# Two more places for raw weight pieces in block one of an attention and expert kernel

## The chip, the cores and the metric

One core of a Trainium2 chip runs the kernel. The metric is the device time of one execution in microseconds (us). The kernel before takes 918.38 us, the median of three runs (917.42 to 919.25).

## What is computed

```python
def _attn_ref(q, k, v):                      # B 4, H 8, S 576, D 64
    q_d, k_d, v_d = (mean over groups of 4 tokens)
    out_up = np.repeat(sm_attn(q_d, k_d, v_d), 4, axis=2)
    mask = np.abs(pos[:, None] - pos[None, :]) < 4
    scores = np.where(mask, scale * q @ k^T, -1000000.0)
    return out_up + softmax(scores) @ v

x = attention as 2304 tokens x 512
h = x @ w_in;  g = relu(h) ** 2;    x = g @ w_out      # block one, d_ff 2048
h = x @ w_in2; g = h * np.cos(h);   out = g @ w_out2   # block two, d_ff 2048
```

The weights come as 64-bit floats. Products in float32 accuracy are made on TensorE of a high part (fp32r) and a low part (the rest): high times high, low times high, high times low.

## The kernel before, in words

**Stages.** First an early stage does pooled ("down") and banded ("pair") attention for the first tokens. Then block one runs in five windows j of 460 or 464 tokens and 16 pieces f of d_ff: slot i = 16 j + f. A slot is `stage_a1` (L801: 12 matmuls into the one bank `ps_h`, xh·w1hi, xl·w1hi, xh·loa), then on ScalarE `gt` = relu (L825), square (L826) and `gh` (L813), on VectorE `gl` = gt - gh (L819), and `stage_b1` (L884: 12 matmuls into `acc`, gh·w1hi, gl·w1hi, gh·lob). "Group f" below is the xh·w1hi and xl·w1hi products of slot f, "gl(f)" its low part. Block two follows (L836, L908). The attention tasks for later windows run in between the slots of block one: scores (L564), exponentials (L386), divisions on GpSimd (L491 for pair, L423 for down), transposes (L503, L433), pooling of the next batch from `pl` tiles (VectorE L368 qc, L373 kp, L375 vp).

**Weights of block one.** Each piece (1 MB of raw 64-bit words, w_in and w_out) is converted once, in the first window, by the task `conv1(f)`. It needs a free `raw` tile (two of them, `caps["raw"]`), loads the piece with one DMA on SyncE's queue (L649), and runs `split`: ScalarE reads the top words (L666), VectorE clamps and shifts (L670, L673) and joins them with the low words (L675, the last reader of `raw`, after which the tile is free again), ScalarE rounds to the high part `w1hi` (L684, into tile `hi{f}`), VectorE subtracts for `loa` and `lob` (L691), which SyncE writes to memory for later windows (L719). `conv1(0)` to `conv1(2)` are tasks from the start; `conv1(f)` starts at slot f - 4.

**Tiles lent out.** The 16 tiles `hi0` to `hi15` are empty until their piece is converted. In the early stage hi3 to hi15 serve as staging for attention inputs: `need` and `done` take them from the list `spare` and put them back; `kept` holds a few for bands.

**What sets the order.** A scheduler builds one instruction list for each engine when the program is made; at run time each engine, and SyncE's queue of DMAs, takes its list strictly in order. All loads and writes that matter here stand on SyncE's queue. Tasks take tiles when `advance` steps them, sorted by `RANK` (attention first, conversions last).

Of the kernel before, what the change touches and what calls it, by code (L numbers as in the profile page):

```python
# [8 lines left out]
F32 = mybir.dt.float32  # L9
F32R = mybir.dt.float32r  # L10
BF16 = mybir.dt.bfloat16
U32 = mybir.dt.uint32
# [6 lines left out]
P = 128  # L19
# [40 lines left out]
TOP_MAX = (2.0 - 2.0 ** -3 - 2.0 ** -23) * 2.0 ** 16 * TOP_SCALE  # L60
LO_RING = (("loa", AHEAD), ("lob", AHEAD + LAG))
SPREAD = ("qk0", "pl", "dpr", "dpt")
LENT = {"dpr": "vw", "dpt": "pl"}
PRODUCTS = ((5, 5), (0, 0), (3, 6), (1, 1), (4, 4), (2, 2), (6, 3))
RANK = {"down": 0, "pair": 1, "pool": 2, "conv1": 3, "conv2": 3}
# [27 lines left out]
def kernel(  # L93
# [76 lines left out]
    def done(name, n=1):  # L170
        f = taken[name].pop(0) if early[0] and name in SPREAD else None
        if f is None:
            used[name] -= n
        elif f in caps:
            used[f] -= n
        else:
            spare.append(f)

    spare = list(range(AHEAD, NF))
    kept = [spare.pop() for _ in range(W0[1] // 4 + 1)]  # L180
    held, taken = {}, {}

# [464 lines left out]
    def load_raw(layer, f):  # L647
        raw = rawp.tile([P, 2 * DM, 2], U32, tag="raw", name="raw")
        nc.sync.dma_start(out=raw.rearrange("p c w -> p (c w)"), in_=weights[layer][f])  # L649
        return raw  # L650

    def behind(*names):
        for name in names:
# [5 lines left out]
        return tc.issue_after(last["pe"]) if follows and not early[0] else nullcontext()  # L659

    def split(raw, hi, los=None, sums=None, held_back=None):
        low, top = raw[:, :, 0], raw[:, :, 1]
        x = rawp.tile([P, 2 * DM], U32, tag="bits", name="bits")
        xv = x.bitcast(F32)
        with behind("hi", "xh", "exp"):
            nc.scalar.activation(out=xv, in_=top.bitcast(F32), func=AF.Prelu, scale=TOP_SCALE, alpha=TOP_ALPHA)  # L666
        while held_back and held_back():
            yield
        with behind("pr" if early[0] and not added[0] else "gl", "xl"):
            nc.vector.tensor_scalar(  # L670
                out=xv, in0=xv, scalar1=TOP_MAX, scalar2=-TOP_MAX * TOP_ALPHA, op0=ALU.min, op1=ALU.max
            )
        nc.vector.tensor_scalar(out=x, in0=x, scalar1=3, scalar2=None, op0=ALU.logical_shift_left)  # L673
        yield
        joined = nc.vector.scalar_tensor_tensor(  # L675
            out=x, in0=low, scalar=29, in1=x, op0=ALU.logical_shift_right, op1=ALU.bitwise_or
        )
        if held_back and added[0]:
            last["xl"] = joined.ins
        if sums:  # L680
            yield from sums(xv)
        yield "read"
        with behind("hi", "xh"):
            nc.scalar.activation(out=hi, in_=xv, func=AF.Copy)  # L684
        yield
        if los is None:
            nc.gpsimd.tensor_tensor(out=xv, in0=xv, in1=hi.bitcast(F32), op=ALU.subtract)
        else:
            for k, lo in enumerate(los()):
                cs = slice(k * DM, (k + 1) * DM)  # L690
                nc.vector.tensor_tensor(out=lo, in0=xv[:, cs], in1=hi[:, cs].bitcast(F32), op=ALU.subtract)  # L691
        return xv
# [2 lines left out]
    lo1 = {}  # L695
    
    def conv1(f, after=0):
        yield from need("raw")
        raw = load_raw(1, f)
        yield  # L700
        yield
        while len(ready) < after or len(scored) < 4:
# [7 lines left out]

        waits = {0: lambda: divided[0] < W0[1], 1: lambda: len(ready) < W0[1]}
        for said in split(raw, hi1[f], ring, held_back=waits.get(f) if early[0] else None):
            if said:
                done("raw")
            yield
            while f == 2 and said and now[0] < 1:
                yield
# [12 lines left out]
    def conv2(u):  # L730
# [4 lines left out]
        yield  # L735
        hi = rawp.tile([P, 2 * DM], F32R, tag="shi", name="shi", bufs=1)
        n = 3 * HALF
        rest = raw.rearrange("p c w -> p (c w)")
        total, top = rest[:, :n].bitcast(F32), rest[:, 2 * DM:2 * DM + n].bitcast(F32R)

        def sums(x):
# [540 lines left out]
```

## Time and profile before

| | before |
|---|---|
| median of 3 runs | 918.38 us (917.42 to 919.25) |
| profiled execution, own time | 915.9 us |
| its span | 914.1 us |
| mean granted clock of TensorE | 0.990 |
| busy: TensorE, VectorE, ScalarE, GpSimd | 891.4, 645.6, 573.0, 97.7 us |

The span is the time from the first to the last instruction that the hardware profiler recorded. TensorE is busy nearly throughout; so what counts is each place where it stands still, what released it there, and the clock that it was granted afterwards. A row of the timeline gives, in brackets, the idle time just before an instruction and what ended it.

### The profile page before, as it was taken

The page shows a single profiled execution, that of the slowest core. Times are in us where ns is not written, and L with a number is a line of the kernel's source. Part 1 is how long each engine was busy: PE and PEld are TensorE (multiplying, and loading weights), DVE is VectorE, ACT ScalarE, POOL GpSimd, SP SyncE. Part 2 cuts the span into 40 slices and gives each one's busy share as a digit, 9 for nine tenths or more (in the row PEclk, how much of TensorE's full clock was granted, in tenths as well). Part 3 has the DMA queues.
Part 4 walks back from the last instruction along what each step waited for, and adds up shares of the span by engine and source line. Part 5 has one row for each costly group of instructions (what it writes and reads, how often), then busy time and mean ns, then how long its engine had stood idle before and what let it go on. Part 6 is the DMA issues. An engine that isn't in the chain of part 4 may idle for free.

```text
span 914.1 us, 17776 instructions
## 1 busy us (share of the span) xinstructions
PE 891.4 (98%) x6946; PEld 814.0 (89%) x6946; DVE 645.6 (71%) x1266; ACT 573.0 (63%) x1039; POOL 97.7 (11%) x79
## 2 busy tenths in 40 slices
PE   7799999999999999999999999999999999999997
PEld 5577788888887888889998999999999999999997
DVE  6999897555766657563311188888888887888786
ACT  5677785455645555454534477776777677777774
POOL 2001320122303313221200000000000000000000
PEclk9799999999999999999999999999999999999999
DMA  9588888867898766884897966655666656566663
GB/s 279 185 324 306 285 305 286 285 254 256 300 331 282 266 231 213 310 307 172 287 386 239 355 222 204 203 187 191 203 202 200 200 200 196 190 196 205 209 227 104
DMA packets 72903, 223.55 MB, mean 245 GB/s; under 512 B 9620, under 2 KB 14612, under 8 KB 68724
## 3 DMA queue, kind: packets, MB, share of 16 engines
q1 hardware_dynamic: 72820, 222.43, 71.5%
q8 instruction: 54, 0.88, 0.4%
q14 instruction: 29, 0.24, 0.1%
HBM read 181.50 MB, written 40.89 MB: 243 GB/s over the span
## 4 chain that ended last, share of the span: by engine, by line
PE 84%; DMA 9%; DVE 3%; ACT 2%; SPq 1%; issue 1%; POOL 0%; DVEq 0%; ACTq 0%; POOLq 0%
PE ps_h L836 22%; PE acc L908 19%; PE ps_h L801 19%; PE acc L884 18%; DMA pl<-in_pool_qk_dram 3%; DMA pl<-in_pool_v_dram 3%; DMA raw<-in_w_dram 2%; DMA pv<-in_pool_v_dram 1%; PE ps_a L412 1%; PE ps_a L606 1%; PE ps_a L564 1%; PE ps_a L449 1%; PE acc L906 1%; PE ps_a L503 1%; PE ps_a L433 1%
## 5 line engine op out<-in xcount | busy, mean ns | idle before, releaser
L836 PE MATMUL ps_h<-x,w2hi 128*128 128x256 f32 x1152 | 160.1, 281 | 0.0
L819 DVE TENSOR_TENSOR gl<-gt,gh 128x460 fp32r<-128x460 f32 (+1 forms) x80 | 59.0, 738 | 141.1 <-ACT gh L813 79.5
L836 PEld LDWEIGHTS ps_h<-x,w2hi 128*128 128x128 f32 x1152 | 146.9, 188 | 0.1
L908 PE MATMUL acc<-bl,gh 128*128 128x256 f32 x504 | 140.6, 280 | 0.0
L801 PE MATMUL ps_h<-xh,w1hi 128*128 128x460 f32 (+1 forms) x320 | 123.3, 386 | 7.4 <-ACT gt L825 3.7
L884 PE MATMUL acc<-gl,w1hi 128*128 128x460 f32 (+1 forms) x320 | 120.5, 377 | 0.2 <-DVE gl L819 0.2
L801 PE MATMUL ps_h<-xl,w1hi 128*128 128x460 f32 (+1 forms) x320 | 120.5, 377 | 0.0
L825 ACT ACTIVATE gt<-ps_h 128x460 f32<-128x460 f32 (+1 forms) x80 | 44.2, 554 | 104.3 <-PE ps_h L801 104.1
L884 PE MATMUL acc<-gh,w1hi 128*128 128x460 f32 (+1 forms) x320 | 107.2, 376 | 0.0
L884 PE MATMUL acc<-gh,lo 128*128 128x460 f32 (+1 forms) x256 | 95.3, 372 | 0.0
L908 PEld LDWEIGHTS acc<-bl,gh 128*128 128x128 f32 x504 | 94.8, 188 | 0.0
L876 DVE TENSOR_TENSOR gl<-g,gh 128x896 fp32r<-128x896 f32 x72 | 78.2, 1087 | 11.0 <-ACT gh L871 11.0
L844 ACT ACTIVATE u<-ps_h,quarter 128x512 f32<-128x512 f32 x72 | 49.4, 687 | 52.6 <-PE ps_h L836 52.4
L908 PE MATMUL acc<-w2hi,gh 128*128 128x256 f32 x288 | 80.7, 280 | 0.0
L908 PE MATMUL acc<-w2hi,gl 128*128 128x256 f32 x288 | 80.2, 280 | 0.0
L851 DVE SCALAR_TENSOR_TENSOR r<-u,ps_h 128x512 f32<-128x512 f32 x72 | 49.4, 687 | 41.3 <-ACT u L846 40.5
L801 PEld LDWEIGHTS ps_h<-xh,w1hi 128*128 128x128 f32 x320 | 60.7, 190 | 17.1 <-ACT gt L825 5.1
L871 ACT ACTIVATE gh<-g 128x896 fp32r<-128x896 f32 x72 | 68.1, 945 | 10.2 <-DVE g L869 10.2
L856 ACT ACTIVATE r<-r,half_pi 128x512 f32<-128x512 f32 x72 | 51.8, 720 | 34.7 <-DVE r L852 34.7
L836 PE MATMUL ps_h<-x,w2lo 128*128 128x256 f32 x432 | 68.5, 280 | 0.0
L884 PEld LDWEIGHTS acc<-gl,w1hi 128*128 128x128 f32 x320 | 60.1, 188 | 7.6 <-DVE gl L819 1.2
L801 PEld LDWEIGHTS ps_h<-xl,w1hi 128*128 128x128 f32 x320 | 60.8, 190 | 6.2
(147 smaller groups left out, 1903.0 us busy)
## 6 DMA issues: line engine op xcount, KB each, us to landing
bl<-wo_d SPq DMA_DIRECT2D x70, 896.0 KB
raw<-in_w_dram SPq DMA_DIRECT2D x32, 1024.0 KB
lo<-lo_d SPq DMA_DIRECT2D x128, 256.0 KB
qkw<-in_win_qk_dram SPq DMA_DIRECT2D x16, 512.0 KB
pl<-in_pool_qk_dram SPq DMA_DIRECT2D x24, 288.0 KB
wo_d<-raw SPq DMA_DIRECT2D x16, 384.0 KB
out_dram<-o SPq DMA_DIRECT2D x18, 256.0 KB
vw<-in_win_v_dram SPq DMA_DIRECT2D x16, 256.0 KB
```

The source lines that it names most:

```text
L412: last["pe"] = nc.tensor.matmul(sv[:, m], qf[:, m * QROWS:(m + 1) * QROWS], kp[:, hp], start=True, stop=True).ins
L801: nc.tensor.matmul(h[:, :n], a[:, c * P:(c + 1) * P], x[:, c, :n], start=i == 0, stop=i == len(order) - 1)
L819: last["gl"] = nc.vector.tensor_tensor(out=gl, in0=gt, in1=gh.bitcast(F32), op=ALU.subtract).ins
L825: last["relu"] = nc.scalar.activation(out=gt, in_=h, func=AF.Relu).ins
L836: nc.tensor.matmul(h[:, s * TB:(s + 1) * TB], a[:, c * P:(c + 1) * P], x[:, c], start=i == 0, stop=i == len(order) - 1,)
L844: nc.scalar.activation(out=u, in_=h, func=AF.Identity, bias=quarter, scale=float(1.0 / (2 * math.pi)))
L851: nc.vector.scalar_tensor_tensor(out=r, in0=u, scalar=-PI2_HI, in1=hv, op0=ALU.mult, op1=ALU.add)
L856: nc.scalar.activation(out=r, in_=r, func=AF.Sin, bias=half_pi, scale=1.0)
L871: nc.scalar.activation(out=gh, in_=g[:, 1:], func=AF.Copy)
L876: nc.vector.tensor_tensor(out=gl, in0=g[:, 1:], in1=gh.bitcast(F32), op=ALU.subtract)
L884: nc.tensor.matmul(acc[d][:, :n], a, x, start=f == 0 and i == 0, stop=f == NF - 1 and i == 2)
L908: nc.tensor.matmul(o, a[:, x], b, start=opens and i == 0, stop=p == NP2 - 1 and i == 2 and (k % 2 == 1 or k == NPROD - 1),)
```

## The change

A piece of block one can now also be loaded into two of the tiles hi12 to hi15 while these are still empty. `done` puts these four, when staging gives them back, on the list `vacant` (`NSPARE` = 2 pairs). `raw_place` takes a raw tile if one is free, and otherwise two vacant tiles with numbers above the piece's own. `load_spare` loads the piece there as two halves of 128x1024 words, one DMA each; `split` then reads the halves with two instructions on ScalarE and two joins on VectorE. After the join the tags go back to `vacant`. The staging tiles are handed out in the reverse order, hi15 first.

```diff
--- before.py
+++ after.py
@@ -60,6 +60,7 @@
 TOP_MAX = (2.0 - 2.0 ** -3 - 2.0 ** -23) * 2.0 ** 16 * TOP_SCALE
 LO_RING = (("loa", AHEAD), ("lob", AHEAD + LAG))
 SPREAD = ("qk0", "pl", "dpr", "dpt")
+NSPARE = 2
 LENT = {"dpr": "vw", "dpt": "pl"}
 PRODUCTS = ((5, 5), (0, 0), (3, 6), (1, 1), (4, 4), (2, 2), (6, 3))
 RANK = {"down": 0, "pair": 1, "pool": 2, "conv1": 3, "conv2": 3}
@@ -174,9 +175,10 @@
         elif f in caps:
             used[f] -= n
         else:
-            spare.append(f)
-
-    spare = list(range(AHEAD, NF))
+            (vacant if f >= NF - 2 * NSPARE else spare).append(f)
+
+    vacant = []
+    spare = list(range(NF - 1, AHEAD - 1, -1))
     kept = [spare.pop() for _ in range(W0[1] // 4 + 1)]
     held, taken = {}, {}
 
@@ -647,7 +649,28 @@
     def load_raw(layer, f):
         raw = rawp.tile([P, 2 * DM, 2], U32, tag="raw", name="raw")
         nc.sync.dma_start(out=raw.rearrange("p c w -> p (c w)"), in_=weights[layer][f])
-        return raw
+        return [(slice(0, 2 * DM), raw)]
+
+    def load_spare(f, tags):
+        parts = []
+        for k, t in enumerate(tags):
+            cs = slice(k * DM, (k + 1) * DM)
+            raw = wp.tile([P, 2 * DM], F32R, tag=f"hi{t}", name="raw").bitcast(U32)
+            nc.sync.dma_start(out=raw, in_=weights[1][f][:, 2 * k * DM:2 * (k + 1) * DM])
+            parts.append((cs, raw.rearrange("p (c w) -> p c w", w=2)))
+        return parts
+
+    def raw_place(f):
+        while True:
+            if used["raw"] < caps["raw"]:
+                used["raw"] += 1
+                return ()
+            mine = [t for t in vacant if t > f]
+            if len(mine) > 1:
+                for t in mine[:2]:
+                    vacant.remove(t)
+                return mine[:2]
+            yield
 
     def behind(*names):
         for name in names:
@@ -659,11 +682,13 @@
         return tc.issue_after(last["pe"]) if follows and not early[0] else nullcontext()
 
     def split(raw, hi, los=None, sums=None, held_back=None):
-        low, top = raw[:, :, 0], raw[:, :, 1]
         x = rawp.tile([P, 2 * DM], U32, tag="bits", name="bits")
         xv = x.bitcast(F32)
         with behind("hi", "xh", "exp"):
-            nc.scalar.activation(out=xv, in_=top.bitcast(F32), func=AF.Prelu, scale=TOP_SCALE, alpha=TOP_ALPHA)
+            for cs, part in raw:
+                nc.scalar.activation(
+                    out=xv[:, cs], in_=part[:, :, 1].bitcast(F32), func=AF.Prelu, scale=TOP_SCALE, alpha=TOP_ALPHA
+                )
         while held_back and held_back():
             yield
         with behind("pr" if early[0] and not added[0] else "gl", "xl"):
@@ -672,9 +697,11 @@
             )
         nc.vector.tensor_scalar(out=x, in0=x, scalar1=3, scalar2=None, op0=ALU.logical_shift_left)
         yield
-        joined = nc.vector.scalar_tensor_tensor(
-            out=x, in0=low, scalar=29, in1=x, op0=ALU.logical_shift_right, op1=ALU.bitwise_or
-        )
+        for cs, part in raw:
+            joined = nc.vector.scalar_tensor_tensor(
+                out=x[:, cs], in0=part[:, :, 0], scalar=29, in1=x[:, cs], op0=ALU.logical_shift_right,
+                op1=ALU.bitwise_or,
+            )
         if held_back and added[0]:
             last["xl"] = joined.ins
         if sums:
@@ -695,8 +722,8 @@
     lo1 = {}
     
     def conv1(f, after=0):
-        yield from need("raw")
-        raw = load_raw(1, f)
+        tags = yield from raw_place(f)
+        raw = load_spare(f, tags) if tags else load_raw(1, f)
         yield
         yield
         while len(ready) < after or len(scored) < 4:
@@ -710,7 +737,9 @@
 
         waits = {0: lambda: divided[0] < W0[1], 1: lambda: len(ready) < W0[1]}
         for said in split(raw, hi1[f], ring, held_back=waits.get(f) if early[0] else None):
-            if said:
+            if said and tags:
+                vacant.extend(tags)
+            elif said:
                 done("raw")
             yield
             while f == 2 and said and now[0] < 1:
@@ -735,7 +764,7 @@
         yield
         hi = rawp.tile([P, 2 * DM], F32R, tag="shi", name="shi", bufs=1)
         n = 3 * HALF
-        rest = raw.rearrange("p c w -> p (c w)")
+        rest = raw[0][1].rearrange("p c w -> p (c w)")
         total, top = rest[:, :n].bitcast(F32), rest[:, 2 * DM:2 * DM + n].bitcast(F32R)
 
         def sums(x):
```

Lines move by this: L649 becomes L651 (whole pieces) and L659 (halves), L666 L689, L675 L701, L684 L711, L691 L718, L719 L748, L801 L830, L819 L848, L825 L854.

**SyncE's queue, loads of pieces 7 and 8.** `raw` is a piece, `pl` an input of pooling, `vw` and `qkw` inputs of pair attention, `lo_d` a write of low parts. Before (raw_995 is piece 7, raw_1091 piece 8):

```order
L649 DMA raw_995<-in_w1_dram 128x2048
L267 DMA pl_871<-in_pool_v_dram 72x512
L512 DMA vw_1199<-in_win_v_dram 128x512
L719 DMA lo_d5_104<-loa_1079 128x512
L719 DMA lo_d5_104<-lob_1080 128x512
L649 DMA raw_1091<-in_w1_dram 128x2048
```

Now (raw_1008 is piece 7, raw_1103 piece 8):

```order
L651 DMA raw_1008<-in_w1_dram 128x2048
L269 DMA pl_881<-in_pool_v_dram 72x512
L269 DMA pl_921<-in_pool_v_dram 72x512
L525 DMA qkw_1298<-in_win_qk_dram 128x1024
L748 DMA lo_d4_103<-loa_931 128x512
L748 DMA lo_d4_103<-lob_932 128x512
L269 DMA pl_923<-in_pool_v_dram 72x512
L269 DMA pl_998<-in_pool_v_dram 72x512
L514 DMA vw_1211<-in_win_v_dram 128x512
L269 DMA pl_1000<-in_pool_v_dram 72x512
L269 DMA pl_1064<-in_pool_v_dram 72x512
L651 DMA raw_1103<-in_w1_dram 128x2048
```

Between the two pieces now stand five more loads of v for pooling and a qkw, and the low parts written there are those of piece 4 instead of 5.

**VectorE ahead of gl(4).** `bits` is a piece under conversion, `vp` pooled v, `xt` the attention output, the last row of each is gl(4). Before, from the join of piece 5 (raw_842):

```order
L675 SCALAR_TENSOR_TENSOR bits_922<-raw_842,bits_922 128x1024
L490 RECIPROCAL mx_974<-mx_974 128x4
L489 TENSOR_SCALAR mx_1042<-mx_1042 128x4
L490 RECIPROCAL mx_1042<-mx_1042 128x4
L373 TENSOR_REDUCE kp_714<-pl_832 128x144
L670 TENSOR_SCALAR bits_991<-bits_991 128x1024
L691 TENSOR_TENSOR loa_1079<-bits_922,w1hi5_921 128x512
L673 TENSOR_SCALAR bits_991<-bits_991 128x1024
L691 TENSOR_TENSOR lob_1080<-bits_922,w1hi5_921 128x512
L623 TENSOR_TENSOR xt_1034<-ps_a_1017,xd_216 128x2x116
L623 TENSOR_TENSOR xt_1034<-ps_a_1016,xd_216 128x2x116
L819 TENSOR_TENSOR gl_1147<-gt_1093,gh_1096 128x460
```

Now, from the second shift of piece 6:

```order
L698 TENSOR_SCALAR bits_1004<-bits_1004 128x1024
L491 TENSOR_SCALAR mx_1055<-mx_1055 128x4
L377 TENSOR_REDUCE vp_723<-pl_923 72x128
L492 RECIPROCAL mx_987<-mx_987 128x4
L377 TENSOR_REDUCE vp_723<-pl_998 72x128
L701 SCALAR_TENSOR_TENSOR bits_1004<-raw_891,bits_1004 128x1024
L492 RECIPROCAL mx_1055<-mx_1055 128x4
L625 TENSOR_TENSOR xt_1047<-ps_a_1030,xd_216 128x2x116
L625 TENSOR_TENSOR xt_1047<-ps_a_1029,xd_216 128x2x116
L718 TENSOR_TENSOR loa_1068<-bits_886,w1hi5_885 128x512
L718 TENSOR_TENSOR lob_1069<-bits_886,w1hi5_885 128x512
L848 TENSOR_TENSOR gl_1159<-gt_1105,gh_1108 128x460
```

The join of piece 6 (raw_891) now stands ahead of gl(4), where it stood behind it, and so do pools of v.

**ScalarE around the rounding of piece 7.** `gt` and `gh` in the first row and below belong to slot 6. Before (raw_1091 is piece 8):

```order
L825 ACTIVATE gt_1296<-ps_h1_1246 128x460
L666 ACTIVATE bits_1203<-raw_1091 128x1024
L826 ACTIVATE gt_1296<-gt_1296 128x460
L684 ACTIVATE w1hi7_1086<-bits_1087 128x1024
L813 ACTIVATE gh_1299<-gt_1296 128x460
L440 COPY dpt_1269<-ps_a_1261 72x288
L666 ACTIVATE bits_1290<-raw_1207 128x1024
```

Now (raw_1103 is piece 8):

```order
L689 ACTIVATE bits_1215<-raw_1103 128x1024
L388 ACTIVATE dpr_1128,dmx_1127<-ps_a_1123,dmx_1127 96x144 x3
L854 ACTIVATE gt_1308<-ps_h1_1258 128x460
L855 ACTIVATE gt_1308<-gt_1308 128x460
L388 ACTIVATE dpr_1169,dmx_1168<-ps_a_1164,dmx_1168 96x144 x3
L842 ACTIVATE gh_1311<-gt_1308 128x460
L711 ACTIVATE w1hi7_1098<-bits_1099 128x1024
L442 COPY dpt_1281<-ps_a_1273 72x288
L711 ACTIVATE w1hi8_1214<-bits_1215 128x1024
```

The conversion of piece 8's top words moved from behind gt of slot 6 to ahead of it; the rounding of piece 7 moved behind gh of slot 6.

## Rows read from the trace of the kernel before

**Rows 1.** Page, part 1: busy time, share, instructions of each engine.

```profile
PE 891.4 (98%) x6946; PEld 814.0 (89%) x6946; DVE 645.6 (71%) x1266; ACT 573.0 (63%) x1039; POOL 97.7 (11%) x79
```

**Rows 2.** Timeline of TensorE, 43 to 102 us: start, duration, instruction, idle before and releaser.

```profile
43.49 0.48 PE L801 MATMUL ps_h<-xh,w1hi 128*128 128x460 f32 x1 [1.84 <-ACT xh L635]
...
49.90 0.47 PE L801 MATMUL ps_h<-xh,w1hi 128*128 128x460 f32 x1 [1.45 <-ACT gt L825]
...
79.16 0.46 PE L884 MATMUL acc<-gl,w1hi 128*128 128x460 f32 x1
...
81.06 0.46 PE L801 MATMUL ps_h<-xh,w1hi 128*128 128x460 f32 x1
...
82.82 1.00 PE L884 MATMUL acc<-gh,w1hi 128*128 128x460 f32 x4
...
89.25 0.63 PE L801 MATMUL ps_h<-xh,w1hi 128*128 128x460 f32 x1 [1.76 <-ACT w1hi L684]
...
92.36 1.22 PE L884 MATMUL acc<-gh,w1hi 128*128 128x460 f32 x4
...
101.64 0.44 PE L503 MATMUL ps_a<-const_sb,pr 128*128 128x128 f32 x2 [1.38 <-POOL pr L491]
```

**Rows 3.** Windows: start:end, length, busy of each engine, PEclk, DMA share, GB/s.

```profile
43.00:50.00 7.00, 5.06 (x23) 3.63 (x23) 6.88 (x10) 3.72 (x7) 0.00 (x0) 0.76 0.19 48
...
89.00:98.00 9.00, 8.75 (x44) 7.39 (x44) 7.40 (x18) 6.26 (x24) 0.00 (x0) 0.81 0.98 360
```

**Rows 4.** Chain of waits in order of time, 80 to 110 us: start, duration, what.

```profile
92.56 1.02 PE acc L884 x4
93.58 0.25 PE ps_a L433 x3
...
94.70 1.67 PE acc L884 x8
96.37 0.75 PE ps_a L412 x6
...
98.08 3.51 POOL pr L491
...
105.42 0.64 PE ps_a L449 x8
```

**Rows 5.** Timeline of ScalarE, 86 to 106 us.

```profile
86.64 1.14 ACT L666 ACTIVATE bits<-raw 128x1024 f32<-128x1024 f32 x1 [1.38 <-DMA raw<-in_w_dram]
...
88.16 1.04 ACT L684 ACTIVATE w1hi<-bits 128x1024 fp32r<-128x1024 f32 x1
...
105.17 1.16 ACT L666 ACTIVATE bits<-raw 128x1024 f32<-128x1024 f32 x1 [0.20 <-DMA raw<-in_w_dram]
```

**Rows 6.** Timeline of SyncE's DMA queue: issues of raw pieces.

```profile
79.05 0.33 SPq L649 DMA_DIRECT2D raw<-in_w_dram  x1
...
99.15 0.35 SPq L649 DMA_DIRECT2D raw<-in_w_dram  x1
```

**Rows 7.** Waits of SyncE's queue, 20 to 145 us: total, times, longest.

```profile
SPq L649 <- DVE bits L675: 43.0, 12, 8.7
```

**Rows 8.** Timeline of GpSimd, 60 us.

```profile
60.03 0.61 POOL L491 TENSOR_TENSOR pr<-pr,mx 128x256 f32<-128x256 f32 x1 [0.95 <-DVE mx L490]
```

**Rows 9.** Groups by line and shape, VectorE, 40 to 160 us: busy, mean ns, idle before.

```profile
L691 DVE TENSOR_TENSOR loa<-bits,w1hi 128x512 fp32r<-128x512 f32 x15 | 10.3, 685 | 0.6 <-ACT w1hi L684 0.6
...
L375 DVE TENSOR_REDUCE vp<-pl 72x128 f32<-72x512 f32 x10 | 6.4, 671 | 0.9 <-DMA pl<-in_pool_v_dram 0.8
```

**Rows 10.** Timeline of VectorE, 64 to 79 us.

```profile
64.84 0.63 DVE L819 TENSOR_TENSOR gl<-gt,gh 128x460 fp32r<-128x460 f32 x1
...
76.71 0.63 DVE L819 TENSOR_TENSOR gl<-gt,gh 128x460 fp32r<-128x460 f32 x1
...
77.77 1.21 DVE L675 SCALAR_TENSOR_TENSOR bits<-raw,bits 128x1024 uint32<-128x1024 uint32 x1
78.91 0.67 DVE L375 TENSOR_REDUCE vp<-pl 72x128 f32<-72x512 f32 x1
```

## The prediction

> **What bounds the kernel now.** I read the page first: TensorE is busy for 891.4 of 914.1 us [rows 1], so a gain can only come out of the 22.7 us in which it idles, or out of stretches at the low clock. The change acts on block one's first window, about 43 to 155 us. There the timeline of TensorE shows where it stood still [rows 2]; the reader is to look at the brackets: 1.84 at 43.49, 1.45 at 49.90, 1.76 at 89.25 and 1.38 at 101.64. The two largest are followed by a lower clock, 0.76 in 43 to 50 and 0.81 in 89 to 98 [rows 3], that is, part of each stretch at 1.2 instead of 2.4 GHz. The price stands in the pitch: eight products take 1.76 at full clock (81.06 to 82.82) and 3.11 after the gap (89.25 to 92.36) [rows 2], and the next four 1.02 by the chain [rows 4] against 0.84, half of the 1.67 that eight take at full clock there [rows 4]. That is 1.35 + 0.18, about 1.55. The gaps of 1.38 and 1.45 cost only themselves: the granted clock did not fall behind them.
>
> Then the cause of the 1.76. ScalarE converts piece 8's top words (L666) at 86.64, after idling 1.38 for that piece's DMA, and only then, at 88.16, rounds piece 7 (L684), for which TensorE waits [rows 5]. Piece 8's load was issued at 79.05 [rows 6]; SyncE's queue had waited for the join of an earlier piece, since there are two raw tiles: 43.0 us over 12 loads [rows 7]. So the raw ring limits this place, through ScalarE's order. At 101.64 the chain shows another limit: one GpSimd division of 3.51 [rows 4], where such a division took 0.61 at 60.03 [rows 8].
>
> What the change can win in the first window is thus 1.76 + 1.55 + 1.38, 4.7 us, and some tenths from smaller gaps: about 5.
>
> **The change, part by part.** By the new order only pieces 1, 2 and 5 of 16 go into the vacant tiles; the rest still use the two raw tiles. SyncE issues three DMAs more, ScalarE and VectorE three instructions more each.
>
> *Halves.* A 128x512 subtraction on VectorE takes 0.685 [rows 9], so two halves of a join are at most 1.37 against 1.21 for the whole [rows 10]: up to 0.16 for each of three pieces. No half-size L666 stands in the trace; at 128x1024 it takes 1.14 [rows 5], and its halves cost between nothing more and, at the 0.685 of the subtraction, 0.23 more. Pieces 1 and 2 are converted beside the early attention work; piece 5 lies in the first window. I put 0.2 on the path (bounds 0 and 1.2, all six instructions exposed).
>
> *Earlier loads of pieces 3 and 4.* Nothing: the gap before piece 3 or 4 is not one that TensorE waits for in rows 2 (it waits for xh and gt there). The cover is the attention work of slots 0 to 3.
>
> *VectorE's order.* Between the low parts gl(2) and gl(4) the old order spends 76.71 - 64.84 = 11.87 us [rows 10]. The new one has five pools of v more (0.60 each: 0.67 long [rows 9], less the 0.07 by which neighbours overlap, as 77.77 + 1.21 and 78.91 do [rows 10]), and the join of piece 6 (about 1.2) ahead of gl(4), and one qc and one kp reduce fewer (taken as 0.67 each, the length of a v pool): 3.0 + 1.2 + 0.1 - 1.35, about 2.95 more. gl(4) then starts at 79.65 and ends about 0.6 later, at 80.25; TensorE first used it at 79.16 [rows 2], with the 0.2 above at 79.36. Stall: up to 0.9; VectorE's own idle time could swallow it all. I take **0.7**, near the upper end, because the v pools wait for loads of their own (0.9 idle in their row [rows 9]).
>
> *Piece 8's load.* It waits for the join of piece 6 on the same raw tile. In the old order that join began at 77.77 and the load left at 79.05 [rows 6, 10]. In the new one it stands ahead of gl(4), with two xt additions and two subtractions behind it (0.6 + 1.2): it ends about 79.65 - 1.8, 77.85. On SyncE's queue it now also stands behind five more v loads and a qkw, the last of which loads waits for the v pool just ahead of that join: no price of its own. So the load leaves only 1.2 earlier. From issue to ScalarE's start took 7.6 for this load and 6.0 for the one at 99.15, at 105.17 [rows 5, 6]; I take 6.75: 84.6. Conversion 1.14, to 85.7; then VectorE's clamps and shifts of pieces 7 and 8 (three at 0.6), a maximum and the join of piece 7, 3.4 in all, to 89.1; rounding 1.0: product group 7 at **90.1**. Before it TensorE now also does four products of group 6 (0.84) that came behind it: its work ends at 87.49 + 0.84 + 0.2 + 0.7 = 89.2. The gap is 0.9 instead of 1.76, **-0.86**, and being under 1.45 it should bring no half clock: **-1.55**.
>
> *The division.* In the new order the reciprocals that feed the two divisions of that slot are followed by maxima and clamps, no longer by a join: **-1.38** (bounds: 0, if it waits as before).
>
> *Group 8.* Its bank comes free when ScalarE has read group 7 (gt), and in the new order the conversion of piece 9 stands ahead of that. Piece 9's load leaves after join 7, at 89.1; + 6.75 + 1.14 + 0.5 for gt: group 8 at 97.5. TensorE's work until then: 90.1 + 1.76 + 0.25 + 1.67 + 0.84 + 0.75 + 0.64 + 0.25 = 96.26 [rows 2, 4]. **+1.3** (0.5 with a landing of 6.0 in both loads, 2.0 with 7.6).
>
> *Later loads.* From about slot 11 on the order is again the old one; piece 9 and later are limited by the same two tiles. Nothing.
>
> **Sum:** 0.2 + 0.7 - 0.86 - 1.55 - 1.38 + 1.3 = -1.6. The profiled execution took 915.9, so 914.3; it lies 2.5 below the median of the runs, 918.38. Shifted by the same: **916.8 us**. With the landings at their ends and the other bounds the forecast's own range is -0.4 to -2.8.
>
> **Rivals.**
> 1. *More of the ceiling.* Group 8 and gl(4) do not wait, because loads land in 6.0 and VectorE takes up the extra pools in its idle time: -2.8 to -5.1, 913.3 to 915.6. For it: slack of 1.9 behind gl(4) today (76.71 + 0.6 to 79.16 [rows 2, 10]). Against: VectorE is what the raw tiles wait for.
> 2. *The wait moves and grows; slower.* Its place is join 6 behind five v pools. If those wait for their loads and piece 8's load leaves at 79.05 or later, it arrives at 86.6 as today; but now conversion, clamps, join 7 and rounding all lie behind it (1.14 + 3.4 + 1.0, where today it is 2.6): group 7 at 92.2. The gap is 92.2 - 89.2 = 3.0, the half clock stays, piece 9's load leaves at 91.2 and group 8 starts at 100.4 at the latest and 99.6 with a quicker landing, against 98.06 in today's timeline (three quarters of a microsecond of other products moved across cancel): +1.5 to +2.3, a second low clock of 1.55 behind that gap, less 1.38 for the division: +1.7 to +3.2 with small changes, 920.1 to 921.6. It decides where the gap passes from 1.45 to 1.76.
> 3. *The half clock alone stays.* The gap at group 7 or 8 lies between 1.45 and 1.76, where no row tells the clock: -1.6 + 1.55, 918.3. This is also where the time lands if the change does in effect not act, since 13 of 16 pieces have the old ring.
> 4. *The division is kept waiting elsewhere.* In the new order four subtractions stand together behind a reciprocal that feeds the down attention's division (L423), whose transposes TensorE wants behind group 7. A held division costs 3.51 - 0.61 = 2.9 [rows 4, 8], of which group 7's 1.76 hides part: 1.15 at most, 917.9. The Trainium skill, SBUF — State Buffer, section Who interferes with whom, says that a VectorE instruction with two SBUF inputs and a GpSimd instruction that reads SBUF exclude each other for a whole instruction; by it these four subtractions would hold the division, and the old 3.51 is such a case. The trace agrees as far as the length goes.
>
> **How the numbers follow.** Chances: forecast 0.44, rival 1 0.22, rival 2 0.24, rival 3 0.06, rival 4 0.04. A change of 0.2%, 1.84 us, is about what a measurement of this kernel can tell from none. Of the forecast's 0.44, 0.18 lies beyond that. Faster: 0.18 + 0.22 = 0.40; slower: 0.24; within: 0.26 + 0.06 + 0.04 = 0.36. The range leaves out the end of rival 1 below -4.6 and the upper part of rival 2 above +2.4, together about 0.15: 913.8 to 920.8.
>
> **What would show it.** Right: piece 8's load leaves near 78; group 7 starts near 90 with a gap under 1.45 before it; the granted clock of 89 to 98 near 1.00; no division wait near 101; a gt wait of about 1.3 before group 8. Wrong: a gap over 1.76 followed by the low clock anywhere in 75 to 110, gl (L819, L848 in the new file) as the releaser of more than 1 us of TensorE, or new gaps before 43 us, where the order is the old one but for the halves and I price nothing.

## The result and the profile after

The changed kernel takes 925.61 us (median of 7 runs, 921.96 to 926.84) against 917.42 for the kernel before (7 runs): a ratio of 1.0081, 95% interval 1.0060 to 1.0102. It is slower by 0.8%, where 916.8 us was forecast and 920.8 was the end of the range. The profiled execution took 922.9 us with a span of 921.1, 7.0 more than before.

Part 1 of the page after. TensorE's busy time is that of [rows 1] within 0.8 us, so nearly all of the loss is idle time, 28.9 against 22.7 us:

```profile
PE 892.2 (97%) x6946; PEld 813.4 (88%) x6946; DVE 647.5 (70%) x1269; ACT 574.0 (62%) x1042; POOL 97.4 (11%) x79
```

TensorE's timeline after shows where it stood still, in the stretch that answers to [rows 2]:

```profile
50.30 0.48 PE L830 MATMUL ps_h<-xh,w1hi 128*128 128x460 f32 x1 [1.71 <-ACT gt L854]
...
59.63 0.44 PE L505 MATMUL ps_a<-const_sb,pr 128*128 128x128 f32 x2 [1.56 <-POOL pr L493]
...
61.86 0.47 PE L913 MATMUL acc<-gl,w1hi 128*128 128x460 f32 x1 [0.95 <-DVE gl L848]
...
79.52 0.59 PE L830 MATMUL ps_h<-xh,w1hi 128*128 128x460 f32 x1 [2.62 <-ACT w1hi L711]
```

And further on in the first window:

```profile
102.22 0.48 PE L830 MATMUL ps_h<-xh,w1hi 128*128 128x460 f32 x1 [0.62 <-ACT gt L854]
...
105.66 0.44 PE L435 MATMUL ps_a<-const_sb,dpr 96*72 96x96 f32 x3 [0.67 <-ACT xd L459]
...
132.30 0.41 PE L435 MATMUL ps_a<-const_sb,dpr 96*72 96x96 f32 x3 [2.22 <-ACT xd L459]
```

The gaps of 1.76 and 1.38 of [rows 2] are gone. In their place stand 1.56, 0.95, 2.62, 0.62, 0.67 and 2.22, which is 8.64 against 3.14. Behind the window lie three of 0.4 or more, 0.61 at 182, 0.45 at 285 and a wait for gt of 1.61 at 289; of these the kernel before has only the last, as 2.00 at 282. The half clock was not saved either, it moved with the large gap from 89 to 80. In the windows view the granted clock is the third number from the end: 0.84 in 80 to 90, in place of 0.81 in 89 to 98 [rows 3].

```profile
80.00:90.00 10.00, 10.00 (x49) 8.64 (x48) 9.60 (x19) 7.04 (x15) 4.41 (x2) 0.84 0.83 269
130.00:140.00 10.00, 7.78 (x50) 6.63 (x44) 9.81 (x17) 7.67 (x16) 0.00 (x0) 1.00 0.67 242
```

The largest gap is before group 5, whose rounding ScalarE began at 78.41 after 1.75 of waiting for the join of piece 5:

```profile
78.41 1.06 ACT L711 ACTIVATE w1hi<-bits 128x1024 fp32r<-128x1024 f32 x1 [1.75 <-DVE bits L701]
```

VectorE's timeline (the two halves of join 5 are the 128x512 row at 77.10, x2; the join of piece 6 is at 80.30) shows what stood ahead of that join:

```profile
67.99 0.75 DVE L375 TENSOR_REDUCE kp<-pl 128x144 f32<-128x576 f32 x1 [0.81 <-DMA pl<-in_pool_qk_dram]
...
72.32 0.63 DVE L848 TENSOR_TENSOR gl<-gt,gh 128x460 fp32r<-128x460 f32 x1
...
75.30 0.68 DVE L377 TENSOR_REDUCE vp<-pl 72x128 f32<-72x512 f32 x1 [2.20 <-DMA pl<-in_pool_v_dram]
...
76.50 0.67 DVE L377 TENSOR_REDUCE vp<-pl 72x128 f32<-72x512 f32 x1
77.10 1.28 DVE L701 SCALAR_TENSOR_TENSOR bits<-raw,bits 128x512 uint32<-128x512 uint32 x2
...
80.30 1.21 DVE L701 SCALAR_TENSOR_TENSOR bits<-raw,bits 128x1024 uint32<-128x1024 uint32 x1
```

gl(3) was done at 72.9. Then VectorE waited 2.20 us for the load of a piece of v, pooled it, clamped piece 6, pooled another piece of v, and only then came to join 5, though nothing of piece 5 was missing but its turn. SyncE's queue tells why that load was late (L266 is q or k for pooling, L269 v, L651 a raw piece):

```profile
62.50 0.33 SPq L266 DMA_DIRECT2D pl<-in_pool_qk_dram  x1
...
66.70 0.33 SPq L651 DMA_DIRECT2D raw<-in_w_dram  x1
68.77 0.91 SPq L269 DMA_DIRECT2D pl<-in_pool_v_dram  x2
...
81.57 0.35 SPq L651 DMA_DIRECT2D raw<-in_w_dram  x1
```

The load of k at 62.50 was pooled at 67.99; only then was one of the two `pl` tiles free for the v loads, which left at 68.77, behind raw piece 7, and arrived at 75.3. Piece 8's load left at 81.57, behind join 6 as the prediction said, but 3.7 us later than it said.

The gap at 132.30 has the same form on ScalarE: the conversion of a raw piece waited for its load, and the copy `xd` that TensorE needs stood behind it and behind a rounding.

```profile
128.97 1.15 ACT L689 ACTIVATE bits<-raw 128x1024 f32<-128x1024 f32 x1 [2.04 <-DMA raw<-in_w_dram]
...
130.46 1.05 ACT L711 ACTIVATE w1hi<-bits 128x1024 fp32r<-128x1024 f32 x1
...
131.88 0.27 ACT L459 COPY xd<-ps_a 128x144 f32<-128x144 f32 x1
```

### The profile page after: what moved, and what is told of

The parts are those of the page before. It is cut to its first block, busy times and chain, and to the rows that moved or that the text cites. A ratio compares the mean times of both kernels' runs of the same rounds, so it can differ in the third digit from the quotient of the medians.

```text
span 921.1 us, 17790 instructions
## 1 busy us (share of the span) xinstructions
PE 892.2 (97%) x6946; PEld 813.4 (88%) x6946; DVE 647.5 (70%) x1269; ACT 574.0 (62%) x1042; POOL 97.4 (11%) x79
## 4 chain that ended last, share of the span: by engine, by line
PE 79%; DMA 10%; DVE 7%; ACT 2%; issue 1%; DVEq 0%; ACTq 0%; SPq 0%
PE ps_h L865 22%; PE acc L937 19%; PE ps_h L830 16%; PE acc L913 15%; DMA pl<-in_pool_v_dram 5%; DMA pl<-in_pool_qk_dram 3%; DMA raw<-in_w_dram 2%; DVE bits L701 1%; DVE vp L377 1%; PE ps_warm L1050 1%; PE ps_a L608 1%; PE ps_a L414 1%; PE acc L935 1%; PE ps_a L451 1%; PE ps_a L566 1%
## 5 line engine op out<-in xcount | busy, mean ns | idle before, releaser
L848 DVE TENSOR_TENSOR gl<-gt,gh 128x460 fp32r<-128x460 f32 (+1 forms) x80 | 60.1, 752 | 142.8 <-ACT gh L842 81.1
L937 PE MATMUL acc<-bl,gh 128*128 128x256 f32 x504 | 140.6, 280 | 0.0
L830 PE MATMUL ps_h<-xh,w1hi 128*128 128x460 f32 (+1 forms) x320 | 123.3, 386 | 9.4 <-ACT gt L854 4.8
L830 PE MATMUL ps_h<-xl,w1hi 128*128 128x460 f32 (+1 forms) x320 | 120.1, 376 | 0.0
L854 ACT ACTIVATE gt<-ps_h 128x460 f32<-128x460 f32 (+1 forms) x80 | 44.2, 554 | 102.9 <-PE ps_h L830 102.7
L937 PEld LDWEIGHTS acc<-bl,gh 128*128 128x128 f32 x504 | 94.7, 188 | 0.0
L937 PE MATMUL acc<-w2hi,gh 128*128 128x256 f32 x288 | 80.7, 280 | 0.0
L937 PE MATMUL acc<-w2hi,gl 128*128 128x256 f32 x288 | 80.2, 280 | 0.0
L830 PEld LDWEIGHTS ps_h<-xh,w1hi 128*128 128x128 f32 x320 | 60.5, 189 | 19.2 <-ACT gt L854 6.2
L913 PEld LDWEIGHTS acc<-gh,w1hi 128*128 128x128 f32 x320 | 60.1, 189 | 7.0 <-ACT gh L842 0.2
```

Of the source, the lines that this page charges most:

```text
L830: nc.tensor.matmul(h[:, :n], a[:, c * P:(c + 1) * P], x[:, c, :n], start=i == 0, stop=i == len(order) - 1)
L848: last["gl"] = nc.vector.tensor_tensor(out=gl, in0=gt, in1=gh.bitcast(F32), op=ALU.subtract).ins
L854: last["relu"] = nc.scalar.activation(out=gt, in_=h, func=AF.Relu).ins
L913: nc.tensor.matmul(acc[d][:, :n], a, x, start=f == 0 and i == 0, stop=f == NF - 1 and i == 2)
L937: nc.tensor.matmul(o, a[:, x], b, start=opens and i == 0, stop=p == NP2 - 1 and i == 2 and (k % 2 == 1 or k == NPROD - 1),)
```

## The experiments

Theory A, formed on this reading: the loss is the new order of the engines' lists, above all VectorE's, where pools whose loads come late stand ahead of joins and of gl. Rivals: B, the halves and their six instructions; C, the reversed staging tiles; D, the traffic of the earlier raw loads. Times below are ratios to the kernel before, run on the same chip.

**1. The reversed tiles alone.**

```diff
-NSPARE = 2
+NSPARE = 0
```

> The changed kernel with no pair of vacant tiles: only the staging tiles are handed out in the reverse order, every piece goes into a raw tile. The instruction lists are those of the kernel before. Theory A (the new order of VectorE's list, pools ahead of joins and of gl, costs the time): as before, 917 to 918 us. Rival B (the halves cost it): as before. Rival C (something of the placing itself, the reversed tiles, costs it): 921 or more.

Measured: 915.83 us, ratio 0.9986 (0.9968 to 1.0004). Rival C is out. Its profile is a second look at the old lists, and it differs from the first where my gain was to come from. TensorE:

```profile
50.20 0.75 PE L830 MATMUL ps_h<-xh,w1hi 128*128 128x460 f32 x1 [1.70 <-ACT gt L854]
...
89.54 0.48 PE L830 MATMUL ps_h<-xh,w1hi 128*128 128x460 f32 x1 [0.29 <-ACT w1hi L711]
```

The granted clock behind group 1, the third number from the end:

```profile
50.00:56.00 6.00, 5.80 (x15) 5.08 (x16) 5.11 (x12) 5.29 (x16) 0.00 (x0) 0.51 1.02 393
```

In the kernel before it is 1.00 in this stretch. There the low clock lay ahead of group 1 (0.59 over 46 to 49); in run 1 it was already low there too (0.50 over 46 to 49) and stayed low behind the gap of 1.70.

The gap before group 7 is 0.29 and not 1.76, with the very same lists, and no low clock follows it (1.00 over 89 to 98). Yet group 7 came no sooner: 45.74 us after group 0 (43.80 to 89.54), against 45.76 in the kernel before (43.49 to 89.25 [rows 2]). Piece 8's load left at 80.25 and ScalarE started on it at 86.91 without waiting, 6.7 us later instead of 7.6 [rows 5, 6], but counted from group 0 that is the same moment, 43.11 against 43.15. What shrank the gap is TensorE: after the low clock behind group 1 it came 1.45 later to group 7 (its work ahead of the gap ends 45.45 after group 0 instead of 44.00).

```profile
80.25 0.33 SPq L651 DMA_DIRECT2D raw<-in_w_dram  x1
```

```profile
86.91 1.15 ACT L689 ACTIVATE bits<-raw 128x1024 f32<-128x1024 f32 x1
```

**2. The halves alone** (on the kernel before, raw tiles as before).

```diff
+        flat = raw.rearrange("p c w -> p (c w)")
+        if layer == 1 and f in (1, 2, 5):
+            parts = []
+            for k in range(2):
+                cs = slice(k * DM, (k + 1) * DM)
+                nc.sync.dma_start(
+                    out=flat[:, 2 * k * DM:2 * (k + 1) * DM], in_=weights[1][f][:, 2 * k * DM:2 * (k + 1) * DM]
+                )
+                parts.append((cs, raw[:, cs]))
+            return parts
...
```

> The kernel before with pieces 1, 2 and 5 still in raw tiles, but loaded by two DMAs of half a piece and read by two instructions on ScalarE and two joins on VectorE, as in the changed kernel. Theory A: the lists keep their order around slots 3 to 6, so at most +1 us, 917.4 to 918.6, and group 5 starts near 75. Rival B (the halves and their six more instructions cost it): 922 or more.

Measured: 920.21 us, ratio 1.0034 (1.0015 to 1.0052): more than A allowed. VectorE's list had moved a little (join 6 stood ahead of gl(4), where it had stood behind it), and the profile shows two gaps close to each other, both released by ScalarE's exponentials:

```profile
95.09 0.98 PE L414 MATMUL ps_a<-kp,qp 128*96 128x144 f32 x6 [1.34 <-ACT pr L388]
96.72 1.23 PE L451 MATMUL ps_a<-dpt,vp 72*64 72x144 f32 x8 [0.65 <-ACT pr L388]
```

These two are not where the time went: counted from group 0, group 16 is only 0.2 later in this profile than in that of the kernel before (109.52 against 109.35). Whether the halves or the small moves cost the 0.34%, run 11 parts.

**3. Two v pools put back behind join 5.**

```diff
+            while b == 1 and not early[0] and isinstance(i, tuple) and "join5" not in last:
+                yield
             while loaded:
...
-        with behind("gl", "xl"):
+        with behind(*(("join5",) if isinstance(piece[0], tuple) else ()), "gl", "xl"):
...
+            if said and f == 5:
+                last["join5"] = last["join"]
...
```

> The changed kernel with one order undone: on VectorE the pools of v for the second window of batch 1 come behind the join of piece 5; all places and halves stay. Theory A: the gap of 2.62 us before group 5 and the half clock behind it go, group 5 starts near 75 instead of 79.5; the whole is 3 to 4 us faster than the changed kernel unless the later order of attention gives it back. Rival D (DMA traffic of the earlier raw loads delays the conversions themselves): group 5 stays near 79, the time stays at 925.

Measured: 923.98 us, ratio 1.0082 (1.0054 to 1.0109), no better than the changed kernel. The place behaved as A said. VectorE came to join 5 at 72.14 instead of 77.10, right behind gl(3):

```profile
71.59 0.63 DVE L853 TENSOR_TENSOR gl<-gt,gh 128x460 fp32r<-128x460 f32 x1
72.14 1.28 DVE L703 SCALAR_TENSOR_TENSOR bits<-raw,bits 128x512 uint32<-128x512 uint32 x2
```

The gap before group 5 and the half clock there were gone. But waits for divisions and for gl opened elsewhere, with one of 2.60 for xt at 159, and in all they took as much:

```profile
61.66 0.75 PE L918 MATMUL acc<-gl,w1hi 128*128 128x460 f32 x1 [1.65 <-DVE gl L853]
...
82.13 0.44 PE L507 MATMUL ps_a<-const_sb,pr 128*128 128x128 f32 x2 [1.48 <-POOL pr L495]
...
89.00 0.44 PE L507 MATMUL ps_a<-const_sb,pr 128*128 128x128 f32 x2 [1.43 <-POOL pr L495]
```

So the gap was understood, and its 2.6 us were not the price of the change: mending one place moved the rest of the lists.

**4. Pooling at half pace** (in the changed kernel), and **8., its control** (the same edit in the kernel before).

```diff
-            for _ in range(1 if b < 2 else 2):
+            for _ in range(1 if b < 1 else 2):
```

> The changed kernel with the pooling of batch 1 at half the pace (a step of two yields for each pair of loads, as batches 2 and 3 have). VectorE's list then has joins 1 to 5 ahead of the pools they stood behind. Theory A: the gaps at 59.6, 61.9 and 79.5 (1.56, 0.95, 2.62) and the half clock go, about 5 to 6 us faster than the changed kernel, 919 to 921, or faster if the earlier pieces now pay. Rivals B and D: no faster than 924.

> Control for the run with paced pools: the kernel before, no vacant tiles, no halves, with the pooling of batch 1 at half the pace. If the 7.2 us that TensorE waits for a window of v near the end of window one in the paced run come from the pace alone, they show here too: 924 or more. If they come from pace and places together, as before within 2 us.

Measured: 928.19 us, ratio 1.0134 (1.0093 to 1.0175), and 927.04 us, 1.0111 (1.0093 to 1.0129). In run 4 the three early gaps went, as expected of A, but the time did not: attention for the next window came late and TensorE waited for its v (column by column: total, times, longest):

```profile
PE ps_a L608 <- DMA vw<-in_win_v_dram: 7.2, 2, 4.4
```

The control has the wait too, so the pace itself costs it, and run 4 says nothing for or against A on the whole:

```profile
170.17 0.47 PE L606 MATMUL ps_a<-pt,vw 64*64 64x56 f32 x4 [4.41 <-DMA vw<-in_win_v_dram]
```

**5. One pair of vacant tiles** (pieces 1 and 5), **6. only pieces 1 and 2**, **7. whole pieces held back**.

```diff
-NSPARE = 2
+NSPARE = 1
```

```diff
-            mine = [t for t in vacant if t > f]
+            mine = [t for t in vacant if t > f and f < AHEAD]
```

```diff
+        if tags:
+            raw = load_spare(f, tags)
+        else:
+            while f >= AHEAD and f - AHEAD not in written:
+                yield
+            with tc.issue_after(written[f - AHEAD]) if f >= AHEAD else nullcontext():
+                raw = load_raw(1, f)
...
+            written[f] = nc.sync.dma_start(out=lo_d[f][:, k * DM:(k + 1) * DM], in_=lo.bitcast(F32)).ins
```

> The changed kernel with one pair of vacant tiles instead of two: pieces 1 and 5 go there, piece 2 into a raw tile. On VectorE joins 5 and 6 now stand ahead of the first pool of v, as they don't in the changed kernel, and no extra reduce stands ahead of gl(1). Theory A (pools ahead of joins and gl): the gaps of 1.56, 0.95 and 2.62 us before 80 us go; 4 us or more faster than the changed kernel, 917 to 921. Rival D (raw traffic): half of the gain at most, 922 or more.

> The changed kernel with the vacant tiles for pieces 1 and 2 alone; piece 5 into a raw tile as before. On VectorE four pools of v stand ahead of joins 5 and 6, as in the changed kernel. Theory A: a gap before group 5 of 2 us or more remains, 923 to 927. Rival E (it is piece 5's early place that costs): as before or up to 920.

> The changed kernel with the loads of whole pieces 3 and later held on SyncE's queue behind the write of the low parts of the piece three before (piece 3 behind the write of 0, piece 6 behind that of 3), near where they were before the change; pieces 1, 2 and 5 keep their early places. Joins 5 and 6 then stand ahead of the pools of v, and gl(1) has no extra reduce ahead. Theory A: no gap over 1.5 before group 5, 4 us or more faster than the changed kernel, 917 to 921. Rival D: as far as raw traffic is what hurts, the traffic is later here too, so this run alone does not part A from D; e5 does. If neither holds (the halves and other moves), 923 or more.

Measured: 924.58 us, 1.0086 (1.0071 to 1.0102); 928.38 us, 1.0133 (1.0103 to 1.0164); 920.91 us, 1.0039 (1.0016 to 1.0061). Run 6 is slower than A said, and slower than with piece 5 in its early place, so rival E is out; its gap before group 5 is 1.03, with 0.99 and 0.51 just ahead of it, not one of 2. Run 7's time is within what A said. It has a longer wait in slot 1 (L861 is gt), which is not the list's, as run 11 below shows:

```profile
50.62 0.75 PE L837 MATMUL ps_h<-xh,w1hi 128*128 128x460 f32 x1 [2.97 <-ACT gt L861]
```

Run 5 missed. The three gaps before 80 us are gone, as A said, and up to group 15 nothing is lost: it begins 99.34 us after group 0, against 99.63 in the kernel before. The same wait in slot 1 is there, but the loss lies behind the first window, where TensorE waits in the attention for the second (group 20 comes 9.2 later than in the kernel before):

```profile
50.83 0.75 PE L830 MATMUL ps_h<-xh,w1hi 128*128 128x460 f32 x1 [2.96 <-ACT gt L854]
```

```profile
176.82 1.01 PE L608 MATMUL ps_a<-pt,vw 64*64 64x56 f32 x26 [4.03 <-DVE xt L625]
```

Runs 3 to 8 show no single place that carries the loss. Each variant gets lists of its own, and each of those waits somewhere, in the first window or behind it. So the next runs changed places and order separately.

**9. to 11. Places and order crossed.** The lists of the two kernels hold the same instructions, halves apart. A table of instruction names in the wanted order was put at the head of the file, and each instruction was tied behind the one before it on its engine, for order alone, without a wait:

```diff
+    traced = nc.cur_bb.bb.instructions
+    by_name = {i.name: i for i in traced}
+    for steps in ORDER:
+        at, names = 0, []
...
+        for a, b in zip(names, names[1:]):
+            tc.add_manual_dep(
+                by_name[b], a, mybir.DependencyInfo(mybir.DependencyClass.NoSync, mybir.DependencyReason.DATA),
+                reason="order of before",
+            )
```

In run 9 the changed kernel has the four compute engines in the old order, with its loads still early; in run 10 the kernel before has them in the new order; in run 11 the changed kernel has SyncE's queue in the old order as well, which runs 9 and 10 leave free.

> The changed kernel (vacant tiles, halves, early loads of pieces 1, 2 and 5, and so of 3 and 4) with the instruction lists of TensorE, VectorE, ScalarE and GpSimd pinned to the order of the kernel before; SyncE's queue free to move the loads ahead. Theory A (the new order of the compute engines costs the time): no gap before groups 3 to 5, 916 to 920, at most the halves' cost of about 3 us above before; the first gap near 89 may shrink. Rivals: if raw traffic (D) or the places themselves cost it, 923 or more in spite of the old order.

> The other corner: the kernel before (two raw tiles, whole pieces, no vacant tiles) with the four compute engines' lists pinned to the order of the changed kernel; SyncE's queue free. Theory A: the gaps of the changed kernel at 59.6, 61.9 and 79.5 are here too, and since the loads are later, larger: 925 or more. Rival D: 917 to 920, since the raw loads are as late as before.

> The changed kernel with all five lists pinned to the order of before, SyncE's too: halves and vacant places, but hardly an earlier load. Price of the halves with no move of order at all: theory A expects 917 to 919; the run with halves alone, 3 us above before, had small moves of order as well, and if the halves themselves cost the 3 us, 920 to 921 here.

| | old order | new order |
|---|---|---|
| two raw tiles, whole pieces | 1 (before) | 1.0104 (1.0083 to 1.0124) |
| vacant tiles, halves, early loads | 1.0000 (0.9986 to 1.0015) | 1.0081 (1.0060 to 1.0102), the change |

Run 11: 0.9987 (0.9972 to 1.0002). This is A, and it excludes B and D: with the old order, places, halves and early traffic cost nothing, and with the new order the kernel without any of them loses as much as the change does. Run 11 also settles run 2: halves with no move of order cost nothing, so the 0.34% there is left to the small moves.

And run 11 settles the wait of 2.97 at slot 1 of runs 5 and 7. With the old order and no loss of time it stands there too (L1301 the groups, L1325 gt):

```profile
50.62 0.75 PE L1301 MATMUL ps_h<-xh,w1hi 128*128 128x460 f32 x1 [2.97 <-ACT gt L1325]
```

Group 1 begins 6.4 to 6.5 us after group 0 in every run but the two with paced pools (here 44.15 to 50.62). Where TensorE ran at the low clock between the two groups its work fills more of that time (gaps of 1.4 to 1.7), where it ran at full clock less (2.9 to 3.0). So the length of this gap says nothing of the lists.

TensorE's gaps in run 9 (the table shifts the lines: L949 are the transposes L503, L1274 the groups L801, L937 the division L491, L1155 the rounding L684):

```profile
59.51 0.44 PE L949 MATMUL ps_a<-const_sb,pr 128*128 128x128 f32 x2 [1.02 <-POOL pr L937]
...
88.19 0.48 PE L1274 MATMUL ps_h<-xh,w1hi 128*128 128x460 f32 x1 [0.29 <-ACT w1hi L1155]
```

And in run 10 (L1245 the groups, L1328 the products with gl, L877 the transposes of down attention, L867 its division):

```profile
50.13 0.75 PE L1245 MATMUL ps_h<-xh,w1hi 128*128 128x460 f32 x1 [2.90 <-ACT gt L1269]
...
64.46 0.48 PE L1328 MATMUL acc<-gl,w1hi 128*128 128x460 f32 x1 [2.37 <-DVE gl L1263]
...
81.55 0.47 PE L1245 MATMUL ps_h<-xh,w1hi 128*128 128x460 f32 x1 [1.03 <-ACT w1hi L1128]
...
100.48 0.70 PE L877 MATMUL ps_a<-const_sb,dpr 96*72 96x96 f32 x3 [3.34 <-POOL dpr L867]
```

Run 10 has gaps before gl(1) (2.37) and group 5 (1.03), where the changed kernel has them too, and one of 3.34 before a transpose of down attention. VectorE had waited 3.56 there for the load of a qc reduce that stands ahead of gl(1), a wait that the changed kernel does not have; that its earlier raw loads make the difference is likely, but not shown. Run 9 shows that they bring nothing with the old order.

**12. and 13. Which list.** The same table for VectorE alone (run 12), and for TensorE, ScalarE and GpSimd with VectorE left free (run 13), both in the changed kernel. In run 13 VectorE's free list again had five pools of v ahead of gl(4), two of them ahead of join 5; it is not the changed kernel's list word for word.

> The changed kernel with VectorE's list alone pinned to the order of the kernel before; TensorE, ScalarE, GpSimd and SyncE free, so that ScalarE may still convert the pieces that arrive early ahead of old work. If VectorE's list is what costs (theory A as stated), 915 to 919, with no gap before groups 3 to 5. If ScalarE's list (conversions ahead of gt and gh) carries the loss, 921 or more.

> The complement: the changed kernel with TensorE's, ScalarE's and GpSimd's lists pinned to the order of the kernel before and VectorE's left to the scheduler, which again puts four pools of v around join 5 and ahead of gl(4). If VectorE's list costs, 921 or more with gaps before groups 3 to 6; if ScalarE's list is the carrier, 915 to 919.

Measured: 920.80 us, ratio 1.0035 (1.0015 to 1.0056), and 925.41 us, 1.0087 (1.0054 to 1.0120). Run 13 is as slow as the change, so a new list on VectorE alone is enough for a loss of this size. Run 12 lies above what A as stated expected: putting VectorE's list back takes away more than half by the medians, not all. What the rest is remains open. The first of its larger gaps is that of slot 1, which is not the list's; the two others are released by ScalarE's exponentials (L922 is gt, L456 the exponentials, L519 and L503 products and transposes of down attention), and at their place run 1, with the old lists, has one of 0.79 (97.43). Run 12:

```profile
50.58 0.75 PE L898 MATMUL ps_h<-xh,w1hi 128*128 128x460 f32 x1 [2.97 <-ACT gt L922]
...
98.44 0.71 PE L519 MATMUL ps_a<-dpt,vp 72*64 72x144 f32 x8 [1.20 <-ACT pr L456]
100.19 0.41 PE L503 MATMUL ps_a<-const_sb,dpr 96*72 96x96 f32 x3 [1.03 <-ACT pr L456]
```

Run 13 (L1291 products with gl, L792 scores of down attention):

```profile
59.94 0.47 PE L1291 MATMUL acc<-gl,w1hi 128*128 128x460 f32 x1 [1.77 <-DVE gl L1226]
...
100.95 1.32 PE L792 MATMUL ps_a<-kp,qp 128*96 128x144 f32 x6 [2.83 <-ACT dpt L820]
```

The two shares, 0.0035 and 0.0087, add up to more than the loss of 0.0081, but by no more than their intervals allow, so whether shares of single lists can be added stays open. No version here is faster than the kernel before by more than its interval.

## Why the prediction was wrong

*What bounds the kernel.* Right in kind: TensorE's gaps in the first window make up most of the difference. Wrong as a gain: the prediction took 0.86 of the 1.76 before group 7, and the 1.55 of half clock behind it, as time that the change wins. Start of the group on TensorE, and in brackets how long after group 0, one profile each:

| | group 0 | group 1 | group 7 | group 8 |
|---|---|---|---|---|
| before | 43.49 | 49.90 (6.41) | 89.25 (45.76) | 98.06 (54.57) |
| run 1, old lists | 43.80 | 50.20 (6.40) | 89.54 (45.74) | 98.28 (54.48) |
| run 11, old order | 44.15 | 50.62 (6.47) | 89.93 (45.78) | 98.57 (54.42) |
| run 9, old order, early loads | 43.44 | 49.91 (6.47) | 88.19 (44.75) | 96.61 (53.17) |
| changed kernel | 43.82 | 50.30 (6.48) | 95.15 (51.33) | 102.22 (58.40) |

Run 1 has 0.29 instead of 1.76 before group 7 and no low clock behind it, and both groups come when they came before. TensorE only reached group 7 later, and ahead of group 8 it waited 0.79 (97.43) and 0.44 (98.28) where in the kernel before it ran its products at the low clock. So the gap and the low clock were slack ahead of the roundings that release these groups (that of piece 8 ends at 98.01 in the kernel before), and which of the two shows was an accident of one execution. What counts is when the rounding ends. Run 9 shows what early loads win there when the order is held: 1.0 at group 7 and 1.4 at group 8. By group 20 nothing of it is left (132.62 after group 0, against 132.68).

*Halves.* Sized at 0.2: run 11 shows nothing that can be measured, and the two half joins of piece 5 took 1.28 together, where 1.37 was the bound. Right.

*Earlier loads of pieces 3 and 4.* Priced at nothing, by the cover of slots 0 to 3. This is a step that failed. The loads themselves cost nothing (run 9), but in the changed kernel there are gaps of 1.56 and 0.95 at 59.63 and 61.86, ahead of group 3, which the prediction left out. For the second, one more qc reduce and a clamp stood ahead of gl(1) on VectorE:

```profile
58.71 0.73 DVE L370 TENSOR_REDUCE qc<-pl 128x144 f32<-128x576 f32 x1
...
60.58 0.68 DVE L695 TENSOR_SCALAR bits<-bits 128x1024 f32<-128x1024 f32 x1
61.18 0.62 DVE L848 TENSOR_TENSOR gl<-gt,gh 128x460 fp32r<-128x460 f32 x1
```

For the first the cause is not shown: run 9, in the old order, waits 1.02 for the same division.

*VectorE's order.* The step that failed most. The sum laid five pools of v end to end at 0.60 and looked only at gl(4), for which it found 0.7. Two things were missing. Join 5, needed for group 5, stands behind two of those pools in the same list; and a pool waits for its load: 2.20 for the first, whose tile came free at 68.7. Together they put join 5 4.78 behind the start of gl(3) (72.32 to 77.10), where run 3, without the pools ahead, has 0.55 (71.59 to 72.14), and the gap before group 5 was 2.62. Run 3 also shows that this one place does not carry the loss; runs 10 and 13 show that such lists as a whole do. The prediction mentioned that pools wait for loads, with 0.9 from the old trace, and took that as a reason for 0.7 instead of following which load, from which queue, into which of two tiles.

*Piece 8's load.* The mechanism (join 6 behind the pools) was right. The load left at 81.57 instead of 77.85, the sum of the same lateness. Group 7 no longer waited for it.

*The division.* Right: no wait near 101. (With the old lists it was 1.38 in one execution and 0.88 in run 1, at 101.35.) A wait of 1.56 for another division came at 59.63. The held division of rival 4 is there too, 3.00 against 0.91 for its like:

```profile
93.96 0.91 POOL L425 TENSOR_TENSOR dpr<-dpr,dmx 96x432 f32<-96x432 f32 x1 [9.55 <-DVE dmx L424]
96.97 3.00 POOL L425 TENSOR_TENSOR dpr<-dpr,dmx 96x432 f32<-96x432 f32 x1 [2.09 <-DVE dmx L424]
```

It lies beside the four subtractions as rival 4 had it, which agrees with the rule of the Trainium skill that rival 4 cites (SBUF — State Buffer, Who interferes with whom), as far as the length goes. It cost TensorE nothing here: no gap names it.

*Group 8.* 1.3 forecast (97.5 less 96.26 is 1.2), 0.62 measured, at 102.22.

*Later loads.* Priced at nothing; the wait for `xd` at 132.30 cost 2.22. Failed in its premise: the order was not again the old one from slot 11 on, which begins at 123.1. ScalarE's list differs from the old one up to 144 us, TensorE's up to 185.

*Rivals.* Rival 2 had the form of what happened: a wait that moves, with a join behind v pools as its place and a gap over 1.76. It was put at piece 6 and group 7; it happened at piece 5 and group 5. Its +1.7 to +3.2 is less than half of the loss, since it was one place, and the timeline shows six. (Its terms add up to +1.7 to +2.5; for the rest no row gives a price.) The prediction also treated the clock as decided by where a gap lies between 1.45 and 1.76; see the last section.

## What to carry to other kernels

When a change frees a buffer and a scheduler makes new lists from it, read for every wait of the critical engine what now stands ahead of its releaser in the list, and what each of those waits for; lay them out with their loads, not with their busy times. Part order from places by pinning the old order onto the new kernel and the new order onto the old one: two runs settled here what the local edits had not. And before a gap is entered as a gain, look at a second execution of the same lists, and count from a common start when the waiting group begins: a gap that shrinks because the engine came later has won nothing.

## What the runs showed of the hardware

The length of a gap alone did not tell what the granted clock did behind it. In the changed kernel and in run 1 alike the clock was 0.50 over 46 to 49, and a gap of 1.71 and one of 1.70 followed ahead of group 1. Behind it the clock was full in the changed kernel:

```profile
50.00:56.00 6.00, 5.70 (x27) 5.17 (x28) 4.39 (x10) 5.54 (x16) 0.00 (x0) 1.00 0.96 339
```

In run 1 it was 0.51 in the same stretch. In run 11 the clock was 1.00 over 46 to 49, the gap 2.97, and the clock behind it low:

```profile
50.00:56.00 6.00, 5.38 (x14) 4.72 (x15) 6.00 (x14) 5.29 (x14) 0.00 (x0) 0.50 0.92 268
```

In the changed kernel the gap of 2.22 at 132.30 was followed by no fall (1.00 over 130 to 140), and the 2.62 at 79.52 by 0.84 over 80 to 90. What else decides is left open; no run here was made for it.
